# GELU as one ScalarE function, the layer norm's g behind the spatial product, w_out in jobs of 256 columns

## Chip, cores and metric

The kernel runs on one core of a Trainium2 chip. The metric is the device time of one execution in microseconds. Before the change it is 832.53 us, the median of three runs (830.43, 832.53 and 833.38).

## What is computed

Hashed attention, followed by a gated MLP with a spatial mixing step. The four batches have 768 positions each, 8 heads of 64, so the MLP sees x of 768 x 512 per batch.

```python
h = x @ w_in                                   # 768x512 @ 512x1024
c = np.float32(np.sqrt(2.0 / np.pi))
h = 0.5 * h * (1.0 + np.tanh(c * (h + 0.044715 * h ** 3)))
u, v = (h[..., :d_ff // 2], h[..., d_ff // 2:])
mu = np.mean(v, axis=-1, keepdims=True)
var = np.mean((v - mu) ** 2, axis=-1, keepdims=True)
v_n = (v - mu) / np.sqrt(var + 1e-06) * g_ln
v_s = np.einsum('ts,bsd->btd', w_sg, v_n) + b_sg[None, :, None]
gated = u * v_s
return (x + gated @ w_out).astype(np.float32)
```

w_in and w_out arrive as 64-bit floats.

## The kernel before

The program has two parts that share one list of jobs. The first is the attention, per pair of heads; it writes its result, transposed, to scratch tiles `xs` in device memory. The second is the MLP, per batch, and the change touches only that one.

Every matmul is made of three with operands split in a high and a low part (`xh`/`xl`, `wih`/`wil`, `zh`/`zl`, `wgh`/`wgl`, `woh`/`wol`, and `gs` twice for the gated values). For a batch, four stages follow each other.

- `load_x` brings four chunks of x; ScalarE makes `xh`, GpSimd `xl`.
- `hidden` first computes six tiles of 128 positions x 512 (the normalised half v): 12 matmuls each into a PSUM buffer `ps_h` (line 765), then GELU into `y`, mean and variance (`bn_stats`, `bn_aggr`, lines 772 and 773), the power -0.5 on GpSimd (775), then subtraction and g (777), the high part `zh` (779, ScalarE) and the low part `zl` (781, VectorE). Then come eight u tiles of 128 x 384 (line 794), which take GELU alone. The `ps_h` buffers are a ring of four, used by both kinds of tiles and by the transposes of `w_sg` (line 724).
- `gate` multiplies w_sg with z, 18 matmuls per half row into one of two `ps_vs` buffers (812), adds the bias b (815), multiplies by u (819), and splits the result (820 ScalarE, 823 GpSimd).
- `project` multiplies by w_out into `ps_o` (838), adds x by four transposing matmuls (843), copies the sum out (847) and stores it. It needs all of `woh` and `wol`.

GELU takes four passes in `gelu2`: a square on ScalarE (749), a VectorE pass that reads it and PSUM (750), a tanh on ScalarE (752), and a VectorE pass that reads it and PSUM once more (754). The factor 0.5 that is missing is made up later: w_out is converted with a factor 0.5, and the variance gets 4e-6 instead of 1e-6.

Beside the first batch, the program also loads g, b and w_sg over ScalarE's DMA queue (`vectors`, `gate_weights`), transposes w_sg (724), splits it (730 and 733), and converts w_out from 64-bit floats (`out_weights`). The conversion is cut in jobs of 128 rows x 128 columns, 16 in all. A job (`weight_job`) is a load on SP's queue (338), seven VectorE steps (356, 357, 359, 361, 362, 363, 365), one GpSimd step (358) and one ScalarE step (364). The scratch tiles `ow64`, `owx`, `owy` and `owg` exist once for all of these jobs, so a load waits until the job before has read its input for the last time (362). The same function converts w_in in 16 jobs of 256 columns during the attention, with scratch tiles `w64`, `wx`, `wy` and `wg`.

The order of instructions on each engine is made by a planner (`Plan.order`): each job has an engine, a cost, a priority and the buffers that it reads and writes; the planner walks through time, and of the jobs that can start it takes the one with the lowest priority number. Costs thus decide the order, on the queues of all engines. An engine then runs its queue strictly in that order.

Of the kernel before, what the change touches and what calls it, by code (L numbers as in the profile page):

```python
# [222 lines left out]
def kernel(  # L223
# [19 lines left out]
    P = 128  # L243
# [501 lines left out]
    def gelu2(ps, dst, n, prio, key=None):

        h2 = tile_of([P, FH], F32, "h2", 2)
        us = n / 960.0
        plan.add(ACT, us - 0.02, prio, lambda: nc.scalar.activation(h2()[:, :n], ps()[:, :n], AF.Square), [ps], [h2])  # L749
        plan.add(DVE, us + 0.07, prio, lambda: nc.vector.scalar_tensor_tensor(  # L750
            h2()[:, :n], h2()[:, :n], 1.0 / GA, ps()[:, :n], op0=ALU.add, op1=ALU.mult), [h2, ps], [h2])
        plan.add(ACT, us - 0.02, prio, lambda: nc.scalar.activation(h2()[:, :n], h2()[:, :n], AF.Tanh, scale=GC * GA),
                 [h2], [h2])
        plan.add(DVE, us + 0.07, prio, lambda: nc.vector.scalar_tensor_tensor(  # L754
            dst(), h2()[:, :n], 1.0, ps()[:, :n], op0=ALU.add, op1=ALU.mult), [h2, ps], [key])

    def hidden(b, xx, prio):
        zh, zl = tile_of([P, NT, FH], F32R, "zh", 1), tile_of([P, NT, FH], F32R, "zl", 1)
        for t in range(NT):
            ps, p0 = ps_of("h", 4), prio + t  # L760
            ts_ = slice(t * P, (t + 1) * P)
            for c, (xh, xl) in enumerate(xx):
                def mm(c=c, xh=xh, xl=xl, ps=ps, ts_=ts_):
                    for n, (x, w) in enumerate(((xh, wih), (xh, wil), (xl, wih))):
# [7 lines left out]
            plan.add(DVE, 0.6, p0, lambda y=y, st=st: V.bn_stats(st(), y()), [y], [st])
            plan.add(DVE, 0.08, p0, lambda st=st, mv=mv: V.bn_aggr(mv()[:, 0:2], st()), [st], [mv])
            plan.add(DVE, 0.08, p0, lambda mv=mv: V.tensor_scalar_add(mv()[:, 2:3], mv()[:, 1:2], 4e-6), [mv], [mv])  # L774
            plan.add(POOL, 0.46, p0, lambda mv=mv: nc.gpsimd.tensor_tensor(mv()[:, 2:3], mv()[:, 2:3], epsr,  # L775
                                                                           op=ALU.pow), [mv], [mv])
            plan.add(DVE, 0.66, p0, lambda y=y, mv=mv: V.scalar_tensor_tensor(
                y(), y(), mv()[:, 0:1], g_bc(), op0=ALU.subtract, op1=ALU.mult), [y, mv, g_bc], [y], port=True)
            plan.add(ACT, 0.6, p0, lambda y=y, mv=mv, t=t: nc.scalar.mul(zh()[:, t, :], y(), mv()[:, 2:3]),  # L779
                     [y, mv], [(zh, t)])  # L780
            plan.add(DVE, 0.66, p0, lambda y=y, mv=mv, t=t: V.scalar_tensor_tensor(  # L781
                zl()[:, t, :], y(), mv()[:, 2:3], zh()[:, t, :].bitcast(F32), op0=ALU.mult, op1=ALU.subtract),
                [y, mv, (zh, t)], [(zl, t)], port=True)
        us = []
        for f in range(NF):
            u = tile_of([P, S], F32, "u", NF)
            fs = slice(f * P, (f + 1) * P)
            for hf in range(2):
                ps, p0 = ps_of("h", 4), prio + 10 + 2 * f + hf
                cs = slice(hf * SH, (hf + 1) * SH)  # L790
                for c, (xh, xl) in enumerate(xx):
                    def mm(c=c, xh=xh, xl=xl, ps=ps, fs=fs, cs=cs):
                        for n, (w, x) in enumerate(((wih, xh), (wih, xl), (wil, xh))):
                            nc.tensor.matmul(ps()[:, :SH], w[:, c, fs], x()[:, cs], start=(c == 0 and n == 0),  # L794
                                             stop=(c == NC - 1 and n == 2))
                    plan.add(PE, 0.49, p0 + 0.01 * c, mm, [xh, xl], [ps])
                gelu2(ps, lambda u=u, cs=cs: u()[:, cs], SH, p0, (u, hf))
            us.append(u)
        return zh, zl, us

    def gate(b, zh, zl, us, prio):
        gs = []
        for f in range(NF):
            fs = slice(f * P, (f + 1) * P)
            gh, gl = tile_of([P, S], F32R, "gs", 2 * NF), tile_of([P, S], F32R, "gs", 2 * NF)
            for hf in range(2):
                cs, p0 = slice(hf * SH, (hf + 1) * SH), prio + 2 * f + hf
                vp, gt = ps_of("vs", 2, (P, SH)), tile_of([P, SH], F32, "gt", 2)
                for t in range(NT):
                    def mm(t=t, vp=vp, fs=fs, cs=cs):  # L810
                        for n, (z, w) in enumerate(((zh, wgh), (zh, wgl), (zl, wgh))):
                            nc.tensor.matmul(vp(), z()[:, t, fs], w()[:, t, cs], start=(t == 0 and n == 0),  # L812
                                             stop=(t == NT - 1 and n == 2))
# [81 lines left out]
```

## Time and profile before

| what | value |
|---|---|
| median of three runs | 832.53 us |
| span of the profiled execution | 833.3 us |
| the run that agrees with that span | 833.38 us |
| attention part, until PE's last sum | 0 to 481.2 us |
| MLP, first batch until its output product starts | 483.5 to 606.6 us |
| rest of the MLP | 606.6 to 829.6 us |
| last copy and store | 829.6 to 833.3 us |
| mean granted clock of PE | 0.983 |

The span runs from the first to the last instruction. PE is the engine of the matmuls, PEld its weight loads, DVE VectorE, ACT ScalarE, POOL GpSimd, SP the engine that issues most DMAs; ACTq and SPq are DMA issues on their queues. A name such as `ps_h` stands for all buffers of that ring. The granted clock is the share of PE's full speed. A wait is put down to the engine and line that ended it.

### The profile page before, as it was taken

What the parts mean: (1) busy time and instruction counts of PE and PEld (TensorE: products, weight loads), DVE (VectorE), ACT (ScalarE), POOL (GpSimd) and SP (SyncE); (2) the same over time, 40 slices, a digit from 0 to 9 for tenths busy, and PEclk for the clock granted to TensorE, in tenths of its full rate; (3) what the DMA queues carried; (4) which work ended last, traced back from release to release, by engine and by line L of the source; (5) the groups of instructions that cost most, each with busy time, mean ns of one, the idle gap of its engine ahead of it and who ended that gap; (6) DMA issues with size and microseconds to landing.
All of it is one profiled execution on the core that took longest, in us unless ns stands there. A gap on an engine that the chain in (4) does not pass through costs nothing.

```text
span 833.3 us, 15304 instructions
## 1 busy us (share of the span) xinstructions
PE 798.5 (96%) x5480; PEld 613.2 (74%) x5480; DVE 595.0 (71%) x1305; ACT 415.7 (50%) x926; POOL 387.2 (46%) x406
## 2 busy tenths in 40 slices
PE   7999999999999999999999986799899999999998
PEld 5776666666666666666666555798689989988996
DVE  7888888888878887988887438889944249416730
ACT  2565665666565655666556645523334135314511
POOL 0656665666667567656767752233204201610130
PEclk9999999999999999999999999799999999999999
DMA  6032323223332331331311155120032230131003
GB/s 155 23 81 69 82 79 99 59 69 93 80 87 62 99 71 50 99 77 53 90 42 50 52 150 177 53 69 26 26 116 94 72 100 1 39 103 49 1 1 126
DMA packets 99307, 60.93 MB, mean 73 GB/s; under 512 B 64288, under 2 KB 91040, under 8 KB 99232
## 3 DMA queue, kind: packets, MB, share of 16 engines
q1 hardware_dynamic: 97920, 56.94, 24.2%
q10 hardware_dynamic: 1312, 3.02, 1.2%
q8 instruction: 43, 0.70, 0.4%
q14 instruction: 32, 0.26, 0.1%
HBM read 47.16 MB, written 12.78 MB: 72 GB/s over the span
## 4 chain that ended last, share of the span: by engine, by line
PE 79%; DVE 14%; DMA 4%; issue 1%; ACT 1%; SPq 0%; ACTq 0%; DVEq 0%
PE g L561 17%; PE av L573 15%; PE ps_vs L812 9%; PE ps_o L838 8%; PE g L517 8%; PE ps_h L794 7%; PE ps_h L765 5%; PE g L497 4%; PE g L475 3%; DVE mx L524 3%; PE g L539 2%; PE g L598 2%; PE ps_o L843 1%; DMA ow<-in_moe_w_out_dram 1%; DMA q<-in_q_dram 1%
## 5 line engine op out<-in xcount | busy, mean ns | idle before, releaser
L582 POOL TENSOR_TENSOR sum<-sum,p 128x384 f32<-128x384 f32 x192 | 196.5, 1045 | 108.2 <-ACT p L567 92.4
L524 DVE TENSOR_REDUCE mx<-g 128x1 f32<-128x384 f32 x384 | 189.3, 550 | 55.0 <-PE g L517 54.4
L567 ACT ACTIVATE p<-g 128x384 f32<-128x384 f32 x384 | 160.4, 495 | 124.8 <-PE g L561 120.8
L573 PE MATMUL av<-p,v 128*64 128x385 f32 x768 | 144.9, 499 | 0.0
L573 PEld LDWEIGHTS av<-p,v 128*64 128x64 f32 x768 | 46.7, 136 | 57.6 <-issue 57.0
L750 DVE SCALAR_TENSOR_TENSOR h<-h,ps_h 128x384 f32<-128x384 f32 (+1 forms) x56 | 33.2, 607 | 67.7 <-ACT h L749 67.5
L561 PE MATMUL g<-hq,hk 64*128 64x384 f32 x384 | 79.4, 391 | 1.7 <-DVE mx L524 1.6
L582 POOL TENSOR_TENSOR sum<-p,p 128x384 f32<-128x384 f32 x64 | 65.0, 1036 | 26.1 <-ACT p L567 26.0
L517 PE MATMUL g<-fk,fq 64*128 64x384 f32 x384 | 73.7, 354 | 3.4 <-DVE mx L524 3.2
L561 PEld LDWEIGHTS g<-hq,hk 64*128 64x128 f32 x384 | 38.5, 184 | 43.4 <-issue 22.3
L517 PE MATMUL g<-hk,hq 64*128 64x384 f32 x384 | 69.2, 338 | 0.0
L561 PE MATMUL g<-hq,lk 64*128 64x384 f32 x384 | 68.0, 336 | 0.0
L561 PE MATMUL g<-fq,fk 64*128 64x384 f32 x384 | 67.9, 335 | 0.0
L561 PE MATMUL g<-lq,hk 64*128 64x384 f32 x384 | 67.7, 335 | 0.0
L775 POOL TENSOR_TENSOR mv<-mv,epsr 128x1 f32<-128x1 f32 x24 | 13.6, 568 | 112.5 <-DVE mv L774 112.5
L838 PE MATMUL ps_o<-woh,gs 128*128 128x512 f32 x192 | 65.5, 402 | 0.0
L812 PE MATMUL ps_vs<-wgh,zh 128*128 128x384 f32 x192 | 64.6, 337 | 0.9 <-ACT zh L779 0.7
L812 PE MATMUL ps_vs<-wgh,zl 128*128 128x384 f32 x192 | 64.4, 335 | 0.7 <-DVE zl L781 0.7
L812 PE MATMUL ps_vs<-wgl,zh 128*128 128x384 f32 x192 | 64.4, 335 | 0.0
L823 POOL TENSOR_TENSOR gs<-gt,gs 128x384 fp32r<-128x384 f32 x32 | 32.5, 1018 | 61.8 <-ACT gs L820 61.8
L794 PE MATMUL ps_h<-xh,wih 128*128 128x384 f32 x128 | 45.6, 356 | 10.1 <-DVE y L754 8.9
L517 PEld LDWEIGHTS g<-fk,fq 64*128 64x128 f32 x384 | 40.2, 185 | 18.5 <-DVE mx L524 11.0
(127 smaller groups left out, 1713.2 us busy)
## 6 DMA issues: line engine op xcount, KB each, us to landing
q<-in_q_dram SPq DMA_DIRECT2D x32, 192.0 KB, 3.6
k<-in_k_dram SPq DMA_DIRECT2D x32, 192.0 KB, 3.2
v<-in_v_dram SPq DMA_DIRECT2D x16, 384.0 KB, 3.3
rs<-r SPq DMA_DIRECT2D x64, 96.0 KB, 3.0
xs<-xt SPq DMA_DIRECT2D x32, 192.0 KB, 1.8
x<-xs SPq DMA_DIRECT2D x16, 384.0 KB, 4.7
rx<-xs SPq DMA_DIRECT2D x96, 64.0 KB, 2.0
out_dram<-ob SPq DMA_DIRECT2D x24, 256.0 KB
```

The lines of the kernel that those rows point to most:

```text
L497: nc.tensor.matmul(fp()[:, :SH], w[:, s, :], x()[:, cs], start=(i == 0), stop=(i == 2))
L517: nc.tensor.matmul(sc[kh][j]()[:, :SH], x[0]()[row(j), qs], x[1]()[row(j), kh * SH:(kh + 1) * SH], start=(n == 0), stop=(n == 1))
L524: plan.add(DVE, 0.56, prio, lambda j=j, kh=kh: nc.vector.tensor_reduce(mx()[:, kh, i, j:j + 1], sc[kh][j]()[:, :SH], axis=AX.X, op=ALU.max ...
L561: nc.tensor.matmul(sc[i][j]()[:, :SH], x()[row(j), ks], y()[row(j), cs], start=(n == 0), stop=(n == 3))
L567: plan.add(ACT, 0.53, prio, lambda i=i, j=j: nc.scalar.activation(p[i][j]()[:, :SH], sc[i][j]()[:, :SH], AF.Exp), [sc[i][j]], [p[i][j]])
L573: nc.tensor.matmul(av()[row(j), :SH + 1], st.v()[:, j, kt, :], p[i][j](), start=(kt == 0), stop=(kt == NT - 1))
L582: (nc.gpsimd if e == POOL else nc.vector).tensor_add(sums[j](), first()[:, :SH], p[i][j]()[:, :SH])
L750: plan.add(DVE, us + 0.07, prio, lambda: nc.vector.scalar_tensor_tensor(h2()[:, :n], h2()[:, :n], 1.0 / GA, ps()[:, :n], op0=ALU.add, op1= ...
L765: nc.tensor.matmul(ps(), x()[:, ts_], w[:, c, FH:FF], start=(c == 0 and n == 0), stop=(c == NC - 1 and n == 2))
L794: nc.tensor.matmul(ps()[:, :SH], w[:, c, fs], x()[:, cs], start=(c == 0 and n == 0), stop=(c == NC - 1 and n == 2))
L812: nc.tensor.matmul(vp(), z()[:, t, fs], w()[:, t, cs], start=(t == 0 and n == 0), stop=(t == NT - 1 and n == 2))
L838: nc.tensor.matmul(po(), a()[:, ts_], w()[:, f, :], start=(f == 0 and n == 0), stop=False)
```

## The change

GELU becomes one ScalarE activation that reads PSUM and writes `y` or `u`. The variance gets 1e-6 and w_out the factor 1.0, since the 0.5 is now inside. The normalised tile is made by one VectorE instruction with two operations, `(y - mean) * rstd`, into a new tile `n`; ScalarE copies `n` to `zh`, VectorE subtracts to `zl`. g is loaded as a column per 128 channels (`g_col`, 512 single values) instead of being broadcast to 128 rows, and multiplies the spatial product in the instruction that adds b. w_out is converted in 8 jobs of 256 columns instead of 16 of 128. Some costs given to the planner are changed too. The core of the diff:

```diff
@@ vectors @@
-        dma(prio, 0.8, lambda eng: eng.dma_start(g_bc(), g_ln.partition_broadcast(P)), w=[g_bc], e=ACT)
+        def columns(eng):
+            with nc.allow_non_contiguous_dma(reason="512 single values"):
+                eng.dma_start(g_col(), g_ln.rearrange("(f p) -> p f", p=P))
+
+        dma(prio, 0.8, columns, w=[g_col], e=ACT)
@@ out_weights @@
-        CO = 128
+        CO = 256
...
-                weight_job(plan, lambda sh, dt, tag: tile_of(sh, dt, "o" + tag, 1), w_out, c, f0, CO, woh, wol, 0.5, prio)
+                weight_job(plan, lambda sh, dt, tag: tile_of(sh, dt, "o" + tag, 1), w_out, c, f0, CO, woh, wol, 1.0, prio)
@@ gelu2 becomes gelu @@
-        plan.add(ACT, us - 0.02, prio, lambda: nc.scalar.activation(h2()[:, :n], ps()[:, :n], AF.Square), [ps], [h2])
-        plan.add(DVE, us + 0.07, prio, lambda: nc.vector.scalar_tensor_tensor(
-            h2()[:, :n], h2()[:, :n], 1.0 / GA, ps()[:, :n], op0=ALU.add, op1=ALU.mult), [h2, ps], [h2])
-        plan.add(ACT, us - 0.02, prio, lambda: nc.scalar.activation(h2()[:, :n], h2()[:, :n], AF.Tanh, scale=GC * GA),
-                 [h2], [h2])
-        plan.add(DVE, us + 0.07, prio, lambda: nc.vector.scalar_tensor_tensor(
-            dst(), h2()[:, :n], 1.0, ps()[:, :n], op0=ALU.add, op1=ALU.mult), [h2, ps], [key])
+    def gelu(ps, dst, n, prio, key):
+
+        plan.add(ACT, n / 1100.0 + 0.17, prio, lambda: nc.scalar.activation(dst(), ps()[:, :n], AF.Gelu_apprx_tanh),
+                 [ps], [key])
@@ hidden @@
+            n = tile_of([P, FH], F32, "n", 2)
...
-            plan.add(DVE, 0.66, p0, lambda y=y, mv=mv: V.scalar_tensor_tensor(
-                y(), y(), mv()[:, 0:1], g_bc(), op0=ALU.subtract, op1=ALU.mult), [y, mv, g_bc], [y], port=True)
-            plan.add(ACT, 0.6, p0, lambda y=y, mv=mv, t=t: nc.scalar.mul(zh()[:, t, :], y(), mv()[:, 2:3]),
-                     [y, mv], [(zh, t)])
-            plan.add(DVE, 0.66, p0, lambda y=y, mv=mv, t=t: V.scalar_tensor_tensor(
-                zl()[:, t, :], y(), mv()[:, 2:3], zh()[:, t, :].bitcast(F32), op0=ALU.mult, op1=ALU.subtract),
-                [y, mv, (zh, t)], [(zl, t)], port=True)
+            plan.add(DVE, 0.42, p0, lambda y=y, mv=mv, n=n: V.tensor_scalar(
+                n(), y(), mv()[:, 0:1], mv()[:, 2:3], op0=ALU.subtract, op1=ALU.mult), [y, mv], [n], port=True)
+            plan.add(ACT, 0.64, p0, lambda n=n, t=t: nc.scalar.copy(zh()[:, t, :], n()), [n], [(zh, t)])
+            plan.add(DVE, 0.69, p0, lambda n=n, t=t: V.tensor_sub(
+                zl()[:, t, :], n(), zh()[:, t, :].bitcast(F32)), [n, (zh, t)], [(zl, t)], port=True)
@@ gate @@
-                plan.add(DVE, 0.47, p0, lambda vp=vp, gt=gt, cs=cs: nc.vector.tensor_add(gt(), vp(), b_bc()[:, cs]),
-                         [vp, b_bc], [gt])
+                plan.add(DVE, 0.55, p0, lambda vp=vp, gt=gt, cs=cs, f=f: nc.vector.scalar_tensor_tensor(
+                    gt(), vp(), g_col()[:, f:f + 1], b_bc()[:, cs], op0=ALU.mult, op1=ALU.add), [vp, b_bc, g_col], [gt])
```

The planner's order is the same in both kernels through the attention and differs behind it. In the rows below, a row is a line of the kernel, an operation, what it writes and reads, and the size; lines of the changed kernel are its own (751 is its GELU, 762 and 790 its v and u matmuls, 834 its output product, 811 and 815 the two gate steps). PE's queue where the first batch's output product (`ps_o`) begins, before:

```order
L794 MATMUL ps_h_8331<-xh_7710,wih 128x384
L794 MATMUL ps_h_8331<-xl_7744,wih 128x384
L794 MATMUL ps_h_8331<-xh_7710,wil 128x384
L838 MATMUL ps_o_8362<-woh_7570,gs_7801 128x512
L838 MATMUL ps_o_8362<-wol_7581,gs_7801 128x512
L838 MATMUL ps_o_8362<-woh_7570,gs_7815 128x512
L838 MATMUL ps_o_8362<-woh_7570,gs_7888 128x512
```

and in the changed kernel:

```order
L762 MATMUL ps_h_7998<-wih,xh_7651 128x512
L762 MATMUL ps_h_7998<-wil,xh_7651 128x512
L762 MATMUL ps_h_7998<-wih,xl_7666 128x512
L762 MATMUL ps_h_8024<-wih,xh_7549 128x512
L762 MATMUL ps_h_8024<-wil,xh_7549 128x512
L762 MATMUL ps_h_8024<-wih,xl_7560 128x512
L834 MATMUL ps_o_8032<-woh_7535,gs_7726 128x512
L834 MATMUL ps_o_8032<-wol_7538,gs_7726 128x512
L834 MATMUL ps_o_8032<-woh_7535,gs_7746 128x512
L834 MATMUL ps_o_8032<-woh_7535,gs_7795 128x512
```

Before, the output product follows the fourth u tile of the second batch (line 794). Now it follows three matmuls of that batch's fifth v tile (line 762), so all u tiles of the second batch and the rest of its v tiles come behind it.

VectorE's queue where the first two gate groups are handled, between jobs of w_out (`ow`, `owx`, `owy`: scratch of a job; `wol`: its result; `gt`: a gate group), before:

```order
L815 TENSOR_TENSOR gt_7792<-ps_vs_7752,b_bc_7453 128x384
L819 TENSOR_TENSOR gt_7792<-gt_7792,u_7504 128x384
L356 TENSOR_SCALAR owy_7803<-ow_5_7778 128x128
L357 SCALAR_TENSOR_TENSOR owx_7808<-ow_5_7778,owy_7803 128x128
L359 SCALAR_TENSOR_TENSOR owx_7808<-owg_7810,owx_7808 128x128
L361 TENSOR_SCALAR owy_7803<-owx_7808 128x128
L362 SCALAR_TENSOR_TENSOR owy_7803<-ow_5_7778,owy_7803 128x128
L363 TENSOR_TENSOR owx_7808<-owx_7808,owy_7803 128x128
L815 TENSOR_TENSOR gt_7833<-ps_vs_7788,b_bc_7453 128x384
L819 TENSOR_TENSOR gt_7833<-gt_7833,u_7504 128x384
L365 SCALAR_TENSOR_TENSOR wol_7581<-owx_7808,woh_7570 128x128
L815 TENSOR_TENSOR gt_7856<-ps_vs_7820,b_bc_7453 128x384
```

and in the changed kernel:

```order
L811 SCALAR_TENSOR_TENSOR gt_7714<-ps_vs_7674,g_col_7421,b_bc_7496 128x384
L815 TENSOR_TENSOR gt_7714<-gt_7714,u_7440 128x384
L356 TENSOR_SCALAR owy_7731<-ow_3_7703 128x256
L357 SCALAR_TENSOR_TENSOR owx_7733<-ow_3_7703,owy_7731 128x256
L811 SCALAR_TENSOR_TENSOR gt_7744<-ps_vs_7710,g_col_7421,b_bc_7496 128x384
L359 SCALAR_TENSOR_TENSOR owx_7733<-owg_7738,owx_7733 128x256
L361 TENSOR_SCALAR owy_7731<-owx_7733 128x256
L362 SCALAR_TENSOR_TENSOR owy_7731<-ow_3_7703,owy_7731 128x256
L363 TENSOR_TENSOR owx_7733<-owx_7733,owy_7731 128x256
L815 TENSOR_TENSOR gt_7744<-gt_7744,u_7440 128x384
L365 SCALAR_TENSOR_TENSOR wol_7538<-owx_7733,woh_7535 128x256
L811 SCALAR_TENSOR_TENSOR gt_7780<-ps_vs_7740,g_col_7421,b_bc_7496 128x384
```

A job of 128 columns stood between two additions (815); a job of 256 columns now stands around the second of two (811), and two additions lie between the first steps of one job and the next.

ScalarE's queue where it issues the loads of b and w_sg (`gs`) in the first batch, before:

```order
L707 DMA gs_0_7413<-in_moe_b_sg_dram 128x768
L752 ACTIVATE h2_4_7369<-h2_4_7369 128x512
L716 DMA gs_1_7419<-in_moe_w_sg_dram 128x768
L752 ACTIVATE h2_5_7387<-h2_5_7387 128x512
L716 DMA gs_2_7425<-in_moe_w_sg_dram 128x768
L716 DMA gs_3_7429<-in_moe_w_sg_dram 128x768
L779 ACTIVATE zh_0_7326<-y_3_7379,mv_3_7400 128x512
L749 ACTIVATE h2_6_7437<-ps_h_6_7364 128x384
```

and in the changed kernel, where `ps_h` numbers tell the tiles:

```order
L707 DMA g_col_0_7421<-in_moe_g_ln_dram 128x4x1
L711 DMA gs_0_7425<-in_moe_b_sg_dram 128x768
L751 ACTIVATE u_0_7440<-ps_h_6_7345 128x384
L720 DMA gs_1_7442<-in_moe_w_sg_dram 128x768
L777 CAST zh_0_7314<-n_4_7433 128x512
L720 DMA gs_2_7449<-in_moe_w_sg_dram 128x768
L751 ACTIVATE u_0_7440<-ps_h_7_7368 128x384
L751 ACTIVATE u_1_7464<-ps_h_8_7391 128x384
L720 DMA gs_3_7470<-in_moe_w_sg_dram 128x768
L751 ACTIVATE u_1_7464<-ps_h_9_7429 128x384
L720 DMA gs_4_7478<-in_moe_w_sg_dram 128x768
```

The loads stood between the passes of GELU and the high parts of z; now they stand between the single GELUs that end the use of a `ps_h` buffer, and the load of g, which stood in the attention's last microseconds, is the first of them.

More of the change, by code (lines that the diff above doesn't have):

```diff
@@ L672 @@
     po_ = Pool("po", "right", PSUM, end)
-    place_of = dict(x=b1, xh=b1, xl=b1, h2=b1, y=b1, st=b1, mv=b1, zh=b2, zl=b2)
+    place_of = dict(x=b1, xh=b1, xl=b1, n=b1, y=b1, st=b1, mv=b1, zh=b2, zl=b2)
     def tile_of(shape, dt, tag, bufs):
@@ L682 @@
     woh, wol = b3.ring([P, NF, DM], F32R, "woh"), b3.ring([P, NF, DM], F32R, "wol")
-    g_bc, b_bc = b2.ring([P, FH], F32, "g_bc"), b3.ring([P, S], F32, "b_bc")
+    g_col, b_bc = b3.ring([P, NF], F32, "g_col"), b3.ring([P, S], F32, "b_bc")
     def dma(prio, us, fn, r=(), w=(), e=SP):
@@ L739, in out_weights @@
     def out_weights(prio):
-        CO = 128
+        CO = 256
         for f0 in range(0, DM, CO):
             for c in range(NF):
-                weight_job(plan, lambda sh, dt, tag: tile_of(sh, dt, "o" + tag, 1), w_out, c, f0, CO, woh, wol, 0.5, prio)
[L745 to L750, printed above, removed]
-            h2()[:, :n], h2()[:, :n], 1.0 / GA, ps()[:, :n], op0=ALU.add, op1=ALU.mult), [h2, ps], [h2])
-        plan.add(ACT, us - 0.02, prio, lambda: nc.scalar.activation(h2()[:, :n], h2()[:, :n], AF.Tanh, scale=GC * GA),
-                 [h2], [h2])
-        plan.add(DVE, us + 0.07, prio, lambda: nc.vector.scalar_tensor_tensor(
-            dst(), h2()[:, :n], 1.0, ps()[:, :n], op0=ALU.add, op1=ALU.mult), [h2, ps], [key])
+                weight_job(plan, lambda sh, dt, tag: tile_of(sh, dt, "o" + tag, 1), w_out, c, f0, CO, woh, wol, 1.0, prio)
+    def gelu(ps, dst, n, prio, key):
+        plan.add(ACT, n / 1100.0 + 0.17, prio, lambda: nc.scalar.activation(dst(), ps()[:, :n], AF.Gelu_apprx_tanh),
+                 [ps], [key])
     def hidden(b, xx, prio):
@@ L769, in hidden @@
             st, mv = tile_of([P, 6], F32, "st", 3), tile_of([P, 3], F32, "mv", 3)
-            gelu2(ps, y, FH, p0, y)
+            gelu(ps, y, FH, p0, y)
+            n = tile_of([P, FH], F32, "n", 2)
             V = nc.vector
[L772 to L775, printed above, removed]
+            plan.add(DVE, 0.69, p0, lambda y=y, st=st: V.bn_stats(st(), y()), [y], [st])
+            plan.add(DVE, 0.18, p0, lambda st=st, mv=mv: V.bn_aggr(mv()[:, 0:2], st()), [st], [mv])
+            plan.add(DVE, 0.15, p0, lambda mv=mv: V.tensor_scalar_add(mv()[:, 2:3], mv()[:, 1:2], 1e-6), [mv], [mv])
+            plan.add(POOL, 0.57, p0, lambda mv=mv: nc.gpsimd.tensor_tensor(mv()[:, 2:3], mv()[:, 2:3], epsr,
                                                                            op=ALU.pow), [mv], [mv])
-            plan.add(DVE, 0.66, p0, lambda y=y, mv=mv: V.scalar_tensor_tensor(
-                y(), y(), mv()[:, 0:1], g_bc(), op0=ALU.subtract, op1=ALU.mult), [y, mv, g_bc], [y], port=True)
-            plan.add(ACT, 0.6, p0, lambda y=y, mv=mv, t=t: nc.scalar.mul(zh()[:, t, :], y(), mv()[:, 2:3]),
-                     [y, mv], [(zh, t)])
-            plan.add(DVE, 0.66, p0, lambda y=y, mv=mv, t=t: V.scalar_tensor_tensor(
-                zl()[:, t, :], y(), mv()[:, 2:3], zh()[:, t, :].bitcast(F32), op0=ALU.mult, op1=ALU.subtract),
-                [y, mv, (zh, t)], [(zl, t)], port=True)
+            plan.add(DVE, 0.42, p0, lambda y=y, mv=mv, n=n: V.tensor_scalar(
[3 more added lines that the diff above has]
+                zl()[:, t, :], n(), zh()[:, t, :].bitcast(F32)), [n, (zh, t)], [(zl, t)], port=True)
         us = []
@@ L796, in hidden @@
                     plan.add(PE, 0.49, p0 + 0.01 * c, mm, [xh, xl], [ps])
-                gelu2(ps, lambda u=u, cs=cs: u()[:, cs], SH, p0, (u, hf))
+                gelu(ps, lambda u=u, cs=cs: u()[:, cs], SH, p0, (u, hf))
             us.append(u)
```

## The prediction

> **What bounds the kernel now.** I read the busy shares first, then a table of stages, then who waited for whom on TensorE (PE), then the chain that ended last.
>
> ```profile
> PE 798.5 (96%) x5480; PEld 613.2 (74%) x5480; DVE 595.0 (71%) x1305; ACT 415.7 (50%) x926; POOL 387.2 (46%) x406
> ```
>
> 96% is an average. The stage table shows, from left to right, the stretch and its length, the busy time (and instructions) of PE, of weight loads, of VectorE (DVE), ScalarE (ACT) and GpSimd (POOL), then the granted PE clock, the DMA share and GB/s.
>
> ```profile
> 483.48:531.70 48.22, 39.26 (x168) 33.42 (x169) 34.37 (x73) 23.70 (x42) 13.71 (x16) 0.89 0.43 127
> 531.70:543.70 12.00, 7.90 (x38) 6.84 (x37) 11.59 (x26) 7.72 (x19) 6.08 (x6) 0.66 0.30 95
> 543.70:606.62 62.92, 58.71 (x291) 53.28 (x290) 57.43 (x148) 19.81 (x43) 18.73 (x26) 0.96 0.12 37
> 606.62:829.64 223.02, 223.01 (x1176) 202.75 (x1175) 98.14 (x185) 77.33 (x139) 46.54 (x45) 1.00 0.20 64
> ```
>
> The attention part ends at 481 us; the program orders it the same in both kernels, so it cancels. From 606.62 to 829.64 PE is busy 223.01 of 223.02 us at clock 1.00: faster vector work is worth nothing there. What can be won lies between 483.48 and 606.62. PE idles there 8.96 + 4.10 + 4.21 = 17.3 us, and the clock is below 1. The waits of PE from 481 to 607 us (total, times, longest) say for whom:
>
> ```profile
> PE ps_h L794 <- DVE y L754: 8.9, 7, 2.6
> PE ps_h L724 <- DVE u L754: 3.5, 1, 3.5
> PE ps_h L765 <- ACT sm L601: 2.3, 1, 2.3
> PE ps_h L765 <- DVE y L754: 1.5, 1, 1.5
> PE ps_h L794 <- DVE u L754: 1.1, 1, 1.1
> ```
>
> Four of the five wait for line 754, the last of the four GELU passes, which gives a PSUM buffer back: 15.0 us. The full-speed length of the same matmuls is read from the last batch, in the chain that ended last (start, length, what):
>
> ```profile
> 751.93 16.80 PE ps_h L765 x72
> 768.73 6.25 PE ps_h L794 x36
> ...
> 786.45 23.94 PE ps_vs L812 x138
> 810.39 2.77 PE ps_o L838 x12
> ...
> 829.19 0.45 PE ps_o L843 x4
> ```
>
> One batch is 829.64 - 751.93 = 77.7 us, four are 310.8. The 36 transposes of the gate weights come on top; the PE timeline has
>
> ```profile
> 536.15 4.42 PE L724 MATMUL ps_h<-ident,gs 128*128 128x128 f32 x18 [3.48 <-DVE u L754]
> ```
>
> so 2 x 4.42 = 8.8. Without loss PE needs 319.6 us from its start at 483.48; it took 829.64 - 483.48 = 346.2. **The loss is 26.5 us**: 17.3 idle and about 9.2 of matmuls stretched by a slow clock. No part of this change can win more than that.
>
> **GELU, per tile.** Durations are the means of groups by line and form (total, mean ns, then idle time before them):
>
> ```profile
> L750 DVE SCALAR_TENSOR_TENSOR h<-h,ps_h 128x512 f32<-128x512 f32 x24 | 16.0, 681 | 45.0 <-ACT h L749 44.8
> L754 DVE SCALAR_TENSOR_TENSOR y<-h,ps_h 128x512 f32<-128x512 f32 x24 | 16.4, 682 | 2.0 <-ACT h L752 1.9
> L772 DVE BATCH_NORM_STATS2 st<-y 128x6 f32<-128x512 f32 x24 | 16.7, 694 | 0.7
> L773 DVE BATCH_NORM_AGGREGATE mv<-st 128x2 f32<-128x6 f32 x24 | 4.3, 178 | 0.4
> L774 DVE TENSOR_SCALAR mv<-mv 128x1 f32<-128x1 f32 x24 | 3.7, 153 | 0.7
> L777 DVE SCALAR_TENSOR_TENSOR y<-y,mv,g_bc 128x512 f32<-128x512 f32 x24 | 17.9, 744 | 0.0
> L781 DVE SCALAR_TENSOR_TENSOR zl<-y,mv,zh 128x512 fp32r<-128x512 f32 x24 | 18.0, 750 | 1.9 <-ACT zh L779 1.9
> L749 ACT ACTIVATE h<-ps_h 128x512 f32<-128x512 f32 x24 | 14.3, 594 | 20.5 <-PE ps_h L765 14.6 <-DVE y L754 5.9
> L752 ACT ACTIVATE h<-h 128x512 f32<-128x512 f32 x24 | 15.0, 632 | 7.4 <-DVE h L750 6.8
> L779 ACT ACTIVATE zh<-y,mv 128x512 fp32r<-128x512 f32 x24 | 17.3, 722 | 13.7 <-DVE y L777 6.1 <-DVE mv L773 4.2 <-DMA gs<-in_moe_b_sg_dram 3.1
> ```
>
> DVE before, per normalised tile: 681 + 682 + 694 + 178 + 153 + 744 + 750 = 3.88 us; PE needs 12 matmuls of 16.80/72 = 0.233, or 2.80. So DVE paces PE. The change removes 681 + 682. The new subtraction-and-scale reads one tensor where L777 read two; L777 bounds it above, half of that is my lower bound. I take the upper end for it and for the low part (750): 2.52 us, under 2.80 even so. ACT: the single GELU lies between one pass (594) and both (594 + 632 = 1226). I take 0.6, the row that also reads PSUM; with the 0.72 copy ACT has 1.3 us per tile, and 1.95 at the upper end, both under 2.80. PE then has the longest of the three, and its PSUM buffer comes back one ACT pass after the last matmul instead of after four passes on two engines. The g multiplication moves into the bias add behind the gate, one pass from PSUM for one pass (L750's kind on the same shape): 0.
>
> A table load precedes the first GELU; the built program has that one and the one at the kernel's start. The only load in the trace, and what ACT does where the new one stands:
>
> ```profile
> L297 ACT ACT_TABLE_LOAD x1 | 1.3, 1283 | 2.0 <-issue 2.0
> 494.42 0.60 ACT L749 ACTIVATE h<-ps_h 128x512 f32<-128x512 f32 x1 [3.36 <-PE ps_h L765]
> ```
>
> 1.28 us lies inside the 3.36 in which ACT waits for PE anyway: 0, and 1.3 if that cover goes. The Trainium skill, page "ScalarE: Activation LUTs", section "What ACT_TABLE_LOAD costs", puts a switch with its drain at about 2.66 us and speaks against mixing sets; by it the cover still holds, with 0.7 us left. No row here shows the drain.
>
> **w_out in 256 columns.** SP's queue, and the DMA list (KB each, median us to landing):
>
> ```profile
> 550.46 50.23 SPq L338 DMA_DIRECT2D ow<-in_moe_w_out_dram  x11
> ow<-in_moe_w_out_dram SPq DMA_DIRECT2D x16, 128.0 KB, 2.2
> w<-in_moe_w_in_dram SPq DMA_DIRECT2D x16, 256.0 KB, 4.1
> ```
>
> A job has one input buffer, so the next load waits for this job's fifth vector step: 49.9/10 = 5.0 us per job now, 16 jobs. The five DVE steps that touch the scratch tile, alone in a stage table, for 16 jobs of 128 columns (w_out, first row) and 16 of 256 (w_in, second):
>
> ```profile
> 483.48:606.62 123.14, 26.09 (x80) 0.90 0.26 78
> 0.00:481.20 481.20, 47.21 (x80) 1.00 0.29 76
> ```
>
> That is 1.63 and 2.95 us per job, so 5.0 = 2.2 landing + 1.63 + 1.17 of other steps between. At 256 the same sum is 4.1 + 2.95 + 1.17 = 8.2 at most: w_in's rows come from the attention part, where more transfers and more POOL work ran beside them. At least it is 6.2, two gate groups of PE work (2 x 18 x 23.94/138), since two groups' additions stand between consecutive jobs on DVE (shown with the change). I take 7.0: 8 jobs of 7.0 for 16 of 5.0.
>
> Why that matters: PE's order puts the first batch's output product in the middle of the second batch's normalised tiles, where it used to follow all of them and half the u tiles. PE gets there near 567 us instead of 606.6, and everything behind it on PE waits. Estimated from the rows above: PE starts at 483.5; 16.8 of normalised tiles, 96 u matmuls of 6.25/36, the slow start and ACT's half microsecond (both below) end near 519; transposes, their wait and a slow stretch near 531.5; eight gate groups of 3.12 near 556.5; 45 matmuls of 0.233 near 567. Job 2 is the last on DVE ahead of the first gate addition (531.5 + 3.1), so job 3's load goes out about 534.6 and job 7 ends about 534.6 + 4 x 7.0 + 7.0 (its own load and steps) = 569.6: a wait of 2 us, within 0 (6.2) and 8 (8.2).
>
> **What remains of the loss.** The clock is also slow after the start's own 2.3 us wait; PE's timeline:
>
> ```profile
> 484.28 0.62 PE L765 MATMUL ps_h<-wih,xh 128*128 128x512 f32 x1
> 484.70 0.63 PE L765 MATMUL ps_h<-wil,xh 128*128 128x512 f32 x1
> ...
> 488.16 0.39 PE L765 MATMUL ps_h<-wil,xh 128*128 128x512 f32 x1
> 488.39 0.39 PE L765 MATMUL ps_h<-wih,xl 128*128 128x512 f32 x1
> ```
>
> 0.42 from start to start against 0.23, for eight matmuls: 1.6 us, which stays. The Trainium skill, page "TensorE: Matmul & The Clock Gate", section "HAM oscillation — how this bites in real kernels", asks for no idle gap above about 3.4 us. The trace is stricter: 2.3 us sufficed. So I count one further slow stretch of 1.6 for the short waits left; by that rule it falls away and the time is 1.6 lower, inside my range (chance 0.2).
>
> The transposes hand their buffers back through ACT and DVE, and one whole w_out job stands between the sixth and seventh of twelve groups on DVE: about 2.5 us, of which PE, running ahead by at most four buffers, sees 0 to 3.6; I take 2. The ACT queue costs 0.5. The sum: 1.6 + 1.6 + 2 + 2 + 0.5 = 7.7 of the 26.5 remain. **Gain 18.8**, so 833.3 becomes 814.5. That execution lies 0.8 above the median of the runs, 832.53; I predict **814 us**.
>
> The new load of g as 512 single values is not in the trace. The nearest is
>
> ```profile
> q<-in_q_dram SPq DMA_DIRECT2D x32, 192.0 KB, 3.6
> ```
>
> with 768 pieces of 256 bytes. I take 3.6 us, from 0 to twice that; it is needed some 25 us after it is issued. The removed broadcast may let x land sooner, 0 to 1 us; I take 0.
>
> **Rivals.** (a) w_out comes late: 8.2 us per job or more, plus a slow clock after the wait, 817 to 824. For it: DVE is busy 57.4 of 62.9 us there. Against: the removed passes take 1.36 us per tile off DVE. Chance 0.14. (b) ACT's own queue becomes the wait. Before,
>
> ```profile
> 510.36 3.61 ACTq L716 DMA_DIRECT2D gs<-in_moe_w_sg_dram  x2
> ```
>
> the second of these loads held ACT until an earlier transfer landed. In the change these loads stand between GELUs, which alone free PSUM now: 3.6 + 1.6 gives 819. Chance 0.1. (c) Slower: the output product moved forward on PE meets weights that are not ready. If half as many jobs take twice as long, the last still ends near 606; PE stands from 567 to 606, and behind it are 19.3 + 2.1 + 2.8 + 16.7 + 25.0 + 19.3 + 155.4 = 240.6 us of matmuls: 606 + 240.6 + 3.7 = 850. It loses to the kernel before only if job 7 ends after 569 + 18.8 = 588, or above 11.6 us per job; the rows give at most 8.2. Chance 0.03. (d) The function is no cheaper than the passes it replaces on ACT: still under PE's 2.80, so 814 to 816; chance 0.03.
>
> **Numbers.** The forecast, 808 to 819, has 0.70. The range for 8 in 10 runs from 807 (only the first slow stretch is left) to 823 (a). 0.3% of this kernel, 2.5 us, is about what a measurement can tell from no change: faster 0.95, same 0.03, slower 0.02.
>
> **What would show it.** PE's waits for the GELU between 483 and 532 us shrink from 15.0 to under 3; transposes start near 519, not 531.7; a w_out load every 6 to 8 us; PE waits at the first output product by 0 to 8 us; from there to the end PE is full. I am wrong if that wait is 15 us or more, or if PE idles in the later batches.

## The result, and the profile after

The changed kernel took 809.95 us (median of four runs, 808.19 to 810.22) against 831.65 us before (four runs on the same chip, 830.43 to 833.38): a ratio of 0.973, with a 95% interval of 0.971 to 0.976. The prediction was 814 us, in a range of 807 to 823. The profiled execution of the change took 808.19 us with a span of 806.4 us. The time lies 1.8 us above the span here, and 1.7 to 1.9 in the profiled executions of the other kernels. So the profile of before, with a span of 833.3, belongs by estimate to an execution of some 835 us, longer than the four listed here, and not to the run of 833.38: the two profiles differ by 26.9 us where the medians differ by 21.7.

First the busy shares of the change, from its page:

```profile
PE 787.3 (98%) x5480; PEld 606.8 (75%) x5480; DVE 520.7 (65%) x1137; ACT 384.1 (48%) x863; POOL 387.1 (48%) x398
```

DVE lost 74 us of work and PE's share rose from 96 to 98%. The stage table has the same columns as the one in the prediction: stretch and length, busy time of PE, weight loads, DVE, ACT and POOL, clock, DMA share, GB/s. The cuts lie shortly before the first transpose (516.08), at the first matmul behind the transposes, at the first output product and behind the last.

```profile
481.56:515.20 33.64, 33.23 (x164) 29.25 (x165) 20.29 (x45) 17.18 (x30) 13.93 (x13) 1.00 0.58 189
515.20:524.43 9.23, 7.00 (x43) 6.66 (x43) 6.94 (x16) 8.02 (x17) 6.28 (x5) 0.95 0.38 119
524.43:562.45 38.02, 38.02 (x196) 35.39 (x196) 34.17 (x69) 8.96 (x20) 15.74 (x17) 0.97 0.18 56
562.45:802.72 240.27, 240.27 (x1270) 219.09 (x1268) 66.05 (x131) 62.98 (x113) 49.60 (x48) 1.00 0.19 60
```

The first row is what was a stretch of 48.22 us at clock 0.89; now it is 33.64 at 1.00. From 524.43 to its last product at 802.72 PE has no idle time. The waits of PE (total, times, longest) in the same part of the program as before:

```profile
PE ps_h L728 <- DVE wgl L737: 2.2, 1, 2.2
PE ps_h L762 <- ACT sm L601: 1.3, 1, 1.3
PE ps_h L762 <- POOL xl L697: 0.4, 1, 0.4
```

None is for the GELU, where it was 15.0 us. The first stands at the transposes of the gate weights. The chain that ended last (start, length, what) shows it, and that the first output product follows the normalised tiles without a gap:

```profile
522.49 0.48 DVE wgl L737
...
523.01 1.42 PE ps_h L728 x6
524.43 2.56 PE ps_h L762 x6
526.98 24.97 PE ps_vs L808 x144
551.95 10.50 PE ps_h L762 x45
562.45 2.77 PE ps_o L834 x12
```

The six normalised matmuls behind the wait take 2.56 us instead of 6 x 0.233 = 1.40: a short low of the clock.

One part of the front moved that the prediction had priced at nothing. PE's first product comes 1.32 us after its last sum product of the attention part, where it had been 2.28, and it runs at full speed at once. The loads of x and what waits for them, on SP's queue and ScalarE, before:

```profile
476.09 0.90 SPq L694 DMA_DIRECT2D x<-xs  x2
476.21 0.35 ACTq L705 DMA_DIRECT2D g_bc<-in_moe_g_ln_dram  x1
480.77 0.83 ACT L699 CAST xh<-x 128x768 fp32r<-128x768 f32 x1 [3.04 <-DMA x<-xs]
```

and after, with PE's start:

```profile
475.14 0.90 SPq L694 DMA_DIRECT2D x<-xs  x2
478.22 0.83 ACT L699 CAST xh<-x 128x768 fp32r<-128x768 f32 x1 [1.44 <-DMA x<-xs]
481.56 0.50 PE L762 MATMUL ps_h<-wih,xh 128*128 128x512 f32 x1 [1.32 <-ACT sm L601]
```

From issue to the cast it was 480.77 - 476.09 = 4.68 us and is now 3.08. In ScalarE's queue the copy of sm, which frees the PSUM buffer that PE's first product takes, stands behind the casts of x; so the earlier x lets PE start earlier.

### The profile page after: what moved, and what is told of

It is laid out like the page before. It is cut to its first block, busy times and chain, and to the rows that moved or that the text cites. A ratio compares the mean times of both kernels' runs of the same rounds, so it can differ in the third digit from the quotient of the medians.

```text
span 806.4 us, 14979 instructions
## 1 busy us (share of the span) xinstructions
PE 787.3 (98%) x5480; PEld 606.8 (75%) x5480; DVE 520.7 (65%) x1137; ACT 384.1 (48%) x863; POOL 387.1 (48%) x398
## 4 chain that ended last, share of the span: by engine, by line
PE 88%; DVE 7%; DMA 2%; POOL 1%; issue 1%; ACT 1%; SPq 0%; DVEq 0%; POOLq 0%; ACTq 0%
PE g L561 17%; PE av L573 15%; PE ps_vs L808 12%; PE ps_o L834 8%; PE g L517 8%; PE ps_h L790 8%; PE ps_h L762 7%; PE g L497 4%; PE g L475 3%; DVE mx L524 3%; PE g L539 2%; PE g L598 1%; PE ps_o L839 1%; DMA q<-in_q_dram 1%; POOL xl L697 1%
## 5 line engine op out<-in xcount | busy, mean ns | idle before, releaser
L811 DVE SCALAR_TENSOR_TENSOR gt<-ps_vs,g_col,b_bc 128x384 f32<-128x384 f32 x32 | 19.7, 616 | 79.9 <-PE ps_vs L808 79.8
L773 POOL TENSOR_TENSOR mv<-mv,epsr 128x1 f32<-128x1 f32 x24 | 16.3, 679 | 99.5 <-DVE mv L772 99.5
L770 DVE BATCH_NORM_STATS2 st<-y 128x6 f32<-128x512 f32 x24 | 16.6, 690 | 67.7 <-ACT y L751 67.7
```

## The experiments

The start of the normalised products varies from run to run by up to 10 us, because the attention part ahead of them does. The experiments are therefore read by a second measure beside the time: the **stretch** from PE's last sum product of the attention part (the last group of L598) to the end of the span. It is 833.3 - 480.66 = 352.6 us before, 806.4 - 479.71 = 326.7 in the change, and 326.9 in a second profile of the change.

Each of the other stretches comes from one profile. Measured against before, the stretch shows a larger gain than the median times in 12 of the 13 profiles below, by 2.4 us on average: this fits before's one profile, which is of an execution longer than its median. A gain against 352.6 may therefore be some 2 us too large; a difference from the change, whose two profiles agree within 0.2, is not touched by that.

The second profile, on the chip of the three edits that follow it, is this run:

> The changed kernel, as it stands, on the same chip as the three edits of it below, so that these have their own base: 0.973 of the kernel before, as measured on another chip; from PE's first product of the layer norm to the end of the span about 324.8 us, of which under 3 us are waits.

Measured: 809.94 us, 0.972 of before (0.967 to 0.977); 325.1 us from the first product. All runs:

| kernel | time, us | ratio to before (95%) | stretch, us |
|---|---|---|---|
| before | 831.7 to 834.6 (medians on four chips) | 1 | 352.6 |
| the change, twice | 809.95, 809.94 | 0.973 (0.971-0.976), 0.972 (0.967-0.977) | 326.7, 326.9 |
| GELU alone | 816.96 | 0.979 (0.975-0.983) | 334.3 |
| g's part alone | 826.98 | 0.994 (0.991-0.996) | 344.6 |
| without w_out's part | 808.01 | 0.969 (0.965-0.973) | 326.3 |
| without g's part | 814.58 | 0.977 (0.973-0.981) | 332.0 |
| without GELU, shared tiles | 843.30 | 1.011 (1.007-1.015) | 358.0 |
| without GELU, in place | 823.65 | 0.991 (0.988-0.994) | 341.6 |
| change + broadcast | 812.06 | 0.975 (0.969-0.981) | 329.9 |
| change + 2 DVE passes, PSUM held | 826.47 | 0.992 (0.989-0.995) | 341.5 |
| change + 2 DVE passes, PSUM free | 831.41 | 0.998 (0.995-1.000) | 346.4 |
| change + 1 DVE pass | 810.26 | 0.973 (0.972-0.975) | 329.4 |
| change, w_out later | 807.72 | 0.970 (0.968-0.973) | 324.1 |

### The parts of the change

GELU alone, without the other two parts:

```diff
-                gelu2(ps, lambda u=u, cs=cs: u()[:, cs], SH, p0, (u, hf))
+                gelu(ps, lambda u=u, cs=cs: u()[:, cs], SH, p0, (u, hf))
```

(and the same for y, with the factor 1.0 in `out_weights` and 1e-6 in the layer norm.)

> The kernel before with one edit: GELU as one ScalarE function (factor 1.0 on w_out, 1e-6 in the layer norm); g stays where it was, w_out stays in 128 columns. Theory A (the gain is the PSUM buffer that comes back after one ScalarE pass instead of four passes on two engines; w_out only has to be in time): nearly all of the gain, 808 to 816 us, no wait of PE for the GELU. Rival C (the larger w_out jobs carry a good part, by relieving DVE and SP between 543 and 607 us): 817 us or more, with PE idle between 543 and 607 us. Rival D (the broadcast of g delayed the load of x): the product of the first tile starts about 1 us later after the attention part than in the change.

Measured: 816.96 us, at the edge between the theories' times (816 and 817). By the signs it is nearer to A: none of PE's waits lies between 543 and 607 us, where rival C wanted them. Rival D came as well: 2.17 us at the start for 1.32. The stretch is 18.3 us shorter than before, of the change's 25.9. The waits of PE in this kernel:

```profile
PE ps_h L724 <- DVE wgl L733: 4.6, 2, 3.6
PE ps_h L758 <- ACT sm L601: 2.2, 1, 2.2
PE ps_h L787 <- ACT u L747: 1.2, 1, 1.2
```

The four passes' wait is gone here too. What is left against the change: the late start (2.2 for 1.3, as in before), more waiting at the transposes (4.6 for 2.2), and 1.2 us for a GELU. That last one is the prediction's rival (b): a load of w_sg holds ScalarE's queue.

```profile
510.18 3.59 ACTq L716 DMA_DIRECT2D gs<-in_moe_w_sg_dram  x2
```

The change without w_out's part (`CO = 128`), and without g's part (`CO = 256` and GELU; g as a broadcast row on the input):

> The change without its last part: w_out in 16 jobs of 128 columns. Theory A: the order of PE puts the first output product after the second batch's normalised and u tiles, about 603 us, and 16 jobs of 5.0 us end by then: 808 to 813 us, the same as the change. Rival C: 816 us or more, with PE waiting for w_out's halves or for DVE between 543 and 607 us.

> The change without its middle part: g again a broadcast row that multiplies the input of the spatial product, on DVE, and loaded by the 256 KB broadcast on ScalarE's queue. Theory A: DVE per normalised tile about 2.5 us, still under PE's 2.80: 809 to 813 us. Theory of the start (the broadcast stood ahead of the load of x): x lands 1 to 2 us later after its issue than in the change, PE waits about 2.3 us instead of 1.3 at the start and has a slow stretch there: about 1 to 2.5 us longer than the change. Rival: the earlier start was chance, and the two agree within 0.5 us at that place.

Measured: 808.01 and 814.58 us, with stretches of 326.3 and 332.0. The first is what theory A gave, the second lies above its 809 to 813. The larger w_out jobs bring nothing as long as g's part is there (326.3 without them, 326.8 with them), and 334.3 - 332.0 = 2.3 us without it. Without g's part PE waits 2.4 us for sm instead of 1.3, as the theory of the start says; at 5.2 us in the stretch (332.0 - 326.8) it costs more than the 1 to 2.5 expected. Two waits that the change does not have are a part of that:

```profile
PE ps_h L787 <- ACT u L747: 1.2, 1, 1.2
PE ps_vs L805 <- DVE gt L808: 0.9, 1, 0.9
```

The first again stands behind two w_sg loads, which held ScalarE's queue for 3.62 us in this kernel.

The change without GELU, in two forms. In the first the subtraction writes into a tile of the ring that the four passes use; in the second in place:

```diff
-            n = tile_of([P, FH], F32, "h2", 2)
+            n = y
```

> The change without its first part: GELU again in four passes over ScalarE and DVE (factor 0.5, 4e-6), with g at the gate and w_out in 256 columns. Theory A: DVE still needs 3.6 us per normalised tile against PE's 2.80 and PSUM comes back late, so PE waits for line y's last pass about as before: 826 to 834 us. Rival C: 822 us or less.

> The change without its first part again, but with the subtraction written in place into the GELU's result tile, so that the layer norm has no third use of the passes' two scratch tiles, which the earlier form of this experiment had. DVE work in the first batch falls by only 6 x (0.74 + 0.75 - 0.55 - 0.72) = 1.3 us against before, and the broadcast is gone: from the last sum product to the end of the span 345 to 352 us against 352.6 before and 326.8 in the change, so 826 to 834 us. If the shared scratch tiles weren't what made the earlier form slow, 356 to 360 again: then the larger w_out jobs cost on DVE as long as the GELU is there.

Measured: 843.30 and 823.65 us, stretches of 358.0 and 341.6. Neither time was expected. The first form is **slower than the kernel before** (by 1.1%), and that goes with the scratch tiles, which three users share there: 16.4 us of the stretch depend on this one line. It says nothing of the change's parts. The second does: without the GELU the other two parts shorten the stretch by 11.0 us (the median times by 8.7), to 3.4 below the least that was expected. So does g's part alone (also in place, w_out in 128 columns):

> The kernel before with only the middle part of the change: g as single values at the gate, subtraction and scale in one pass in place, a copy and a subtraction for the halves; GELU in four passes, w_out in 128 columns. x lands 3.1 us after its issue and PE starts 1.3 us after its last sum product, at full clock. If that start is worth its 3 us here too, the stretch from the last sum product is 348 to 350 us and the time 3 to 4 us under the kernel before; if DVE's work sets the first part of the stretch, the earlier start of PE is lost again in the waits for DVE and the gain is 0 to 2 us.

Measured: 826.98 us, a stretch 8.0 us shorter, more than either theory gave; by the median times the gain is 5.4 us (3.0 to 7.7), which leaves room for the first theory's 3 to 4. The start explains 2.6 of it (below). PE's waits for y's and u's last pass fall from 15.0 to 5.2 us (here L758):

```profile
PE ps_h L797 <- DVE u L758: 2.6, 1, 2.6
PE ps_h L797 <- DVE y L758: 2.6, 2, 2.1
```

DVE's own passes became shorter as well: subtraction and low part took 0.74 and 0.75 us before and take 0.54 and 0.68 here. And the w_sg loads, which held ScalarE for 3.61 us before, pass at once in this kernel (0.39 and 0.33). Which of these brings the rest was not separated.

GELU's 18.3 and g's 8.0 add up to the 26.3 us of both together (352.6 - 326.3); by the median times it is 17.6 and 5.4 against 26.6, within what the intervals leave open. w_out's part adds 3.0 to g's, 2.3 to GELU's and -0.5 to both. That it relieves a DVE which is no longer short of time once both are in would fit; no run shows it by itself.

### The start

The change with one 256 KB transfer put back, which nothing reads:

```diff
+        g_bc = tile_of([P, FH], F32, "n", 2)
+        dma(prio, 0.8, lambda eng: eng.dma_start(g_bc(), g_ln.partition_broadcast(P)), w=[g_bc], e=ACT)
         dma(prio, 0.8, columns, w=[g_col], e=ACT)
```

> The change with one transfer put back: at the old place on ScalarE's queue, ahead of the single values of g, a broadcast of g (256 KB) into a layer-norm tile, which nothing reads. Theory of the start (the broadcast, which goes out 0.1 us after the loads of x, slows them): x lands 4.7 us after its issue instead of 3.1, PE waits 2.2 to 2.4 us for sm instead of 1.3, the clock is low behind that gap, and the kernel takes 2.5 to 4 us more than the change. Rival (the order of the other queues or chance made the difference): 3.1 us and 1.3 us as in the change, and its time within 1 us.

Measured: 812.06 us, 2.1 more than the change on that chip, with intervals that overlap; the profile is plainer. SP's queue, ScalarE's, then PE's timeline:

```profile
475.22 0.90 SPq L694 DMA_DIRECT2D x<-xs  x2
```

```profile
475.33 0.35 ACTq L710 DMA_DIRECT2D n<-in_moe_g_ln_dram  x1
479.88 0.83 ACT L699 CAST xh<-x 128x768 fp32r<-128x768 f32 x1 [3.02 <-DMA x<-xs]
```

```profile
482.58 0.50 PE L764 MATMUL ps_h<-wih,xh 128*128 128x512 f32 x1 [2.27 <-ACT sm L601]
...
483.48 0.63 PE L764 MATMUL ps_h<-wih,xh 128*128 128x512 f32 x1
483.90 0.63 PE L764 MATMUL ps_h<-wil,xh 128*128 128x512 f32 x1
```

x takes 4.66 us again, PE waits 2.27 again, and matmuls follow each other in 0.42 us instead of 0.23, as before the change. The stretch is 3.0 us longer, as the theory of the start said; the time's 2.1 is a little under its 2.5 to 4. That theory is confirmed: with the broadcast issued 0.1 us after the loads of x, the first of them is ready 1.6 us later. Not all of the 3.0 is the start, though. PE's waits here have one that the change does not have:

```profile
PE ps_h L764 <- ACT sm L601: 2.3, 1, 2.3
PE ps_h L792 <- ACT u L753: 0.8, 1, 0.8
```

The start itself is 0.95 us of waiting and some 1.6 of slow matmuls, about 2.6 together; 0.8 is a GELU whose queue w_sg loads held for 1.98 us, and the wait at the transposes is 0.4 shorter (1.8).

### What GELU's four passes cost: held PSUM or DVE's work

Both come with the four passes. Two kernels take them apart. Each adds two DVE passes per GELU tile to the change, which write scratch; the first reads the tile in PSUM as well and so holds it, the second reads only the result:

```diff
+            for _ in range(2):
+                plan.add(DVE, 0.69, p0, lambda y=y, n=n, ps=ps: nc.vector.scalar_tensor_tensor(
+                    n(), y(), 1.0, ps(), op0=ALU.add, op1=ALU.mult), [y, ps], [n])
```

(In the second `y()` for `ps()`; both likewise for the u tiles.)

> The change with two more DVE passes per GELU tile, which read the GELU's result and the tile in PSUM and write into a scratch tile of the layer norm that the subtraction overwrites: PSUM is held as long as by the four passes, but ScalarE does one pass and the result does not wait for them. DVE per normalised tile 2.29 + 2 x 0.68 = 3.65 us, more than PE's 2.80. Both theories: PE waits again for DVE, 8 to 16 us before the transposes, and the time is 12 to 25 us above the change.

> The same two DVE passes, but they read the GELU's result alone, so PSUM comes back after ScalarE's pass. Theory A (the late PSUM buffer is what PE waited for): PE runs ahead over its four buffers and two result tiles, its waits before the transposes stay under 5 us, and the kernel takes 3 to 8 us more than the change. Rival B (DVE's pace of 3.65 us per tile against 2.80 sets it, whoever holds PSUM): waits and time as with PSUM held, within 3 us of that kernel.

Measured: stretches of 341.5 and 346.4 us, times of 826.47 and 831.41. With PSUM held the time is in the expected range and the waits before the transposes, 6.9 us, are a little less than expected. With PSUM free the time is far above theory A's, and 4.9 us above the kernel with PSUM held where rival B allowed 3. The waits of PE, PSUM held:

```profile
PE ps_h L793 <- DVE n L770: 6.7, 3, 3.8
PE ps_h L728 <- DVE wgl L737: 2.8, 2, 2.5
```

PSUM free:

```profile
PE ps_h L728 <- DVE wgl L737: 12.6, 1, 12.6
PE ps_h L728 <- ACT u L751: 2.0, 2, 1.1
PE ps_h L793 <- ACT y L751: 1.9, 2, 1.6
```

With PSUM free PE runs ahead as theory A says: before the transposes (L728) only the 1.9 us of the last row. Then it stands 12.6 us at the transposes, whose copies are queued on DVE behind the extra passes:

```profile
519.95 12.62 DVE L799 SCALAR_TENSOR_TENSOR n<-u 128x384 f32<-128x384 f32 x14
```

These 14 passes take 0.90 us each on average. With PSUM held, passes of the same size take 0.53:

```profile
526.57 5.34 DVE L799 SCALAR_TENSOR_TENSOR n<-u,ps_h 128x384 f32<-128x384 f32 x10
```

So the two kernels do not add the same work. In the first batch the added passes take 16.7 us with PSUM held and 22.5 with PSUM free. Of the 14 passes ten take 0.55 or 0.56 us, as those with PSUM do. The other four (0.97, 2.04, 2.15 and 2.15, from 522.07, 523.07, 525.04 and 528.76) are just those that overlap GpSimd's work on `xl`:

```profile
522.58 4.19 POOL L697 TENSOR_TENSOR xl<-x,xh 128x768 fp32r<-128x768 f32 x2
528.68 1.82 POOL L697 TENSOR_TENSOR xl<-x,xh 128x768 fp32r<-128x768 f32 x1 [1.91 <-ACT xh L699]
```

With PSUM held two passes fall beside the same work of GpSimd (533.72 to 537.34) and take 0.55. So a pass that reads `u` alone was held up beside GpSimd here, and one that reads PSUM as well was not.

The stretch grows by 14.6 us for the 16.7 and by 19.5 for the 22.5: 4.9 more for 5.8 more of DVE's time. So **the time goes by DVE's work, and holding PSUM only decides where PE meets it**. Theory A falls for the time: the returned buffer alone is worth at most about 1 us here (an estimate, 5.8 less 4.9). And the two added passes make up the whole cost of the four: the kernel without GELU, in place, has a stretch of 341.6, the one with two added passes and PSUM held 341.5, so the second pass on ScalarE adds nothing that shows.

One long wait comes with a low clock, 0.79 and 0.61 in the two parts of that stage:

```profile
516.00:531.00 15.00, 5.24 (x30) 4.66 (x28) 14.62 (x21) 5.99 (x12) 7.49 (x5) 0.79 0.27 87
531.00:545.00 14.00, 7.30 (x33) 6.63 (x34) 13.00 (x31) 5.39 (x11) 2.40 (x3) 0.61 0.30 95
```

How much room DVE has was asked with one pass instead of two (`range(1)`, PSUM free):

> The change with one more DVE pass per GELU tile (it reads the GELU's result and writes a scratch tile), instead of two. It adds 6 x 0.68 + 8 x 0.55 = 8.5 us of DVE work in the first batch; two passes added 17.0, and from the last sum product of the attention part to the end of the span they cost 346.4 - 326.9 = 19.5 us. Theory W (what counts is DVE's whole work between the first GELU tile and the last half of the gate weights, against what is left of DVE's idle time there: 1.5 + 0.4 + 3.8 = 5.7 us in the change): most of the 8.5 fits in, PE waits about 5 us at the transposes instead of 2.2, and that stretch is 3 to 5 us longer than 326.9. Theory L (every microsecond of DVE there costs one): 9 to 10 us longer. Theory P (DVE's pace per normalised tile, 2.29 + 0.68 = 2.97 against PE's 2.80): under 1.5 us longer.

Measured: 810.26 us, the change's time (0.973 of before both). The stretch is 2.5 us longer, but PE waits only 1.5 us at the transposes; 1.9 more are a GELU that stood behind a blocked load of w_sg:

```profile
504.62 4.62 ACTq L720 DMA_DIRECT2D gs<-in_moe_w_sg_dram  x2
```

Theory L falls. The 2.5 us lie between theory P (under 1.5) and theory W (3 to 5), and W's 5 us at the transposes did not come, so neither was right. What stands is that the cost is not in proportion: by the traces 8.8 us of added passes in the first batch lengthen the stretch by 2.5 us, 16.7 by 14.6. Most of the first fits into DVE's idle time.

### The change with w_out's jobs later

PE's one wait for DVE in the change was put down in advance to a w_out job between the sixth and seventh copy of the gate weights on DVE. Its priority was moved:

```diff
-MLP = {"xl": "POOL", "gm": "DVE", "gl": "POOL", "wg": 398.29, "wo": 46.93, "x": 568.79}
+MLP = {"xl": "POOL", "gm": "DVE", "gl": "POOL", "wg": 398.29, "wo": 410.0, "x": 568.79}
```

> The change with a later priority for w_out's jobs (410 instead of 46.93), so that on DVE ten of the twelve halves of the gate weights come first and one whole w_out job stands before the last two, and that PE reaches the first output product only after the second batch's normalised and most of its u tiles. If the w_out job in the middle of the halves is what PE's 2.2 us wait at the transposes comes from: that wait goes below 1 us, the stretch from the last sum product is 324 to 326 us, and the time is 1 to 2.5 us under the change's. If the wait has another cause it stays at 2 us and so does the time.

Measured: 807.72 us, 0.970 (0.968 to 0.973). All of PE's waits that are left, and the 36 transposes in one run:

```profile
PE ps_h L762 <- ACT sm L601: 1.3, 1, 1.3
PE ps_h L762 <- POOL xl L697: 1.2, 2, 0.9
```

```profile
520.61 5.68 PE L728 MATMUL ps_h<-ident,gs 128*128 128x128 f32 x36
```

The wait is gone and the stretch 2.7 us shorter than the change's, as expected if the w_out job was its cause. (The edit moves all of w_out's jobs; on DVE ten copies of the gate weights now follow each other.) By time alone this kernel, the change, and the change without w_out's part can't be told apart (their intervals overlap); all three beat the kernel before.

## Why the prediction was right, and where its sum was off

The sign, the place of the gain and the bound were right, and of the mechanism the half that counts: with the four passes gone DVE no longer sets the front, PE does, and the gain comes entirely ahead of the stretch where PE is full. The change came out 4 us faster than predicted by the median, and 8.1 by the spans of the two profiles, because before's profile is of an execution longer than its median and the change's of one shorter than its own. By the prediction's terms:

- **GELU, 15.0 us of waits to 0: right.** So was the new pass at 0.60 (measured 0.596) and the table load at nothing. ScalarE's timeline has it inside a wait for PE, as predicted:

```profile
488.72 1.28 ACT L751 ACT_TABLE_LOAD   x1
491.21 1.30 ACT L751 ACTIVATE y<-ps_h 128x512 f32<-128x512 f32 x2 [1.20 <-PE ps_h L762]
```

- **Why it works: half right.** The prediction named both DVE's 3.88 us per tile against PE's 2.80 and the PSUM buffer that comes back late. Only the first counts: two extra passes cost 14.6 us of stretch for 16.7 us of DVE's time with PSUM held, and 19.5 for 22.5 with PSUM free.
- **The start: a term of the wrong size.** "1.6 slow start" stayed in the sum and the removed broadcast was taken at 0 within 0 to 1. It is worth 2.6 us: 0.96 us less wait for sm (2.28 to 1.32), and 1.6 because behind the shorter wait the clock did not fall. The step that failed was to price the transfer alone and not what stands in ScalarE's queue behind the tile that it delays.
- **g's part: priced at nothing, worth 5.2 us of stretch beside both other parts and 8.0 alone.** Behind the start's 2.6 stand w_sg loads that no longer hold ScalarE's queue, and DVE passes for which the prediction kept the old length as its upper end (0.74 and 0.75 us; 0.55 and 0.72 in the change). How the rest divides between them stays open.
- **The transposes, 2 us of waits: right** (2.2), and so was the cause. **The second slow stretch, 1.6: right**: 2.56 for 1.40 us behind the wait and 1.42 for the last six transposes, which take 6 x 5.68/36 = 0.95 at full speed, together 1.6. By the Trainium skill, page "TensorE: Matmul & The Clock Gate", section "HAM oscillation — how this bites in real kernels", whose rule the prediction cites, only idle gaps above about 3.4 us count, and the term would be nothing; behind this wait of 2.2 us the trace decided against it.
- **w_out, 2 us of waits: 0 came.** SP's queue has five loads from the first to the last issue in 26.5 us, 6.63 per job against the 7.0 taken:

```profile
529.00 26.86 SPq L338 DMA_DIRECT2D ow<-in_moe_w_out_dram  x5
```

DVE's last step of job 7 ends at 562.24 and PE's first output product starts at 562.45. The margin is 0.2 us, so that nothing came of this term is in part luck; it was inside its bounds (0 to 8).
- **ScalarE's queue, 0.5: 0 came**, and 0.4 for another wait (POOL's xl), which was not in the sum. Rival (b) did not occur in the change, but it is real: blocked w_sg loads cost PE 1.2 us with GELU alone, 1.2 without g's part, 0.8 with the broadcast and 1.9 with one more DVE pass.
- **PE's full-speed length, 319.6 us: too long by 3.2.** The transposes were taken at 2 x 4.42 from a stretch where the clock stood at 0.66; at full speed 36 take 5.68 us. So the loss of before was 29.7 us, not 26.5, and the change's is 802.72 - 481.56 - 316.5 = 4.7: 2.2 + 0.4 + 1.6 and half a microsecond not found.

From the predicted span of 814.5 to the 806.4 of the profile these make: start 2.6 (0.96 and 1.6), w_out 2.0, the transposes' length 3.2, and 0.95 by which the attention part happened to end earlier: together 8.7, where 8.1 were measured; the half microsecond not found is most of the difference. All four went the same way, so they did not hide each other. Rivals (a), (c) and (d) did not occur.

## What to carry to other kernels

A PSUM buffer that is returned late and an engine that has too much to do look the same in the list of waits: to find which one sets the time, take the hold away and leave the work, and measure the work that is left, which may not have the same length. Before a lossless length is put together from rows, look up the clock of the stretch that they stand in. A transfer that is removed is priced by the queue that waits for its neighbours, not by its own bytes.

## What was not expected of the hardware

PE's clock fell behind waits of 2.17 to 2.35 us ahead of the first product in all four kernels that have one (before, GELU alone, without g's part, with the broadcast): six to eight matmuls follow at 0.42 us from start to start, then 0.23 again. In all ten profiles with the 1.32 us wait at the same place the matmuls follow at 0.23 at once. And a broadcast of 256 KB on another queue, issued 0.1 us after two loads of 384 KB, made the first of them ready some 1.6 us later: from issue to the cast that reads it pass 4.63 to 4.68 us in all four profiles with it, 2.94 to 3.25 in the ten without.
